# Norm factor moved behind the projections in a two-layer decode kernel

## Chip, cores, metric

The kernel runs on one core of a Trainium2 chip. The metric is device time in microseconds (us). Three runs of the kernel before spread over 0.3% (1176.41 to 1179.94 us), so a few us of 1177 need several runs. The sets of rounds ran on different chips, so compare kernels of different rounds by their ratios to the kernel before.

## The reference, cut to what matters

Two layers, each attention over a cache and then an mlp, for 8 rows of one token. Layernorm stands before every projection, twice in a row before the mlp's.

```python
def _layernorm(x, axis=-1, eps=1e-5):
    m = jnp.mean(x, axis=axis, keepdims=True)
    v = jnp.var(x, axis=axis, keepdims=True)
    return (x - m) / jnp.sqrt(v + eps)

def _A_ref(x, k_cache, v_cache, wq, wo):      # x [8,1,448], caches [8,8,4096,256] bf16
    q = (x @ wq) ...                          # 16 heads of 256
    p = softmax(einsum(q, k) / 16);  o = einsum(p, v)
    return o @ wo
def _B_ref(x, w1, w2, w3, w4):                # with one token the shifted branch adds zeros
    x1 = x + hs                               # hs = 0 here
    return x1 + _gelu(_layernorm(x1) @ w3) @ w4

x = x + _A_ref(_layernorm(x), ...);  x = x + _B_ref(_layernorm(x), ...)   # twice
```

## The kernel before

K and V come in chunks of 1 MB through a ring of five buffers (440 chunks in all). TensorE (PE) transposes K, VectorE (DVE) and ScalarE (ACT) copy the transposes out, PE makes scores and the product with V. Some K of a row stays on chip for the second layer, so that the two layers are interleaved: row b of layer 1 runs beside row b+1 of layer 0. The norm, queries and mlp of a row are generators ("jobs"). A piece of a job, up to its next `yield`, is put into the stream between pieces of attention. The traces show each engine's instructions in the order in which they are written (an example is the copy in the section "The copy to the upper partitions back on PE": it ran at 1167.25 us, with its input there since 1164.83).

The activations are 448 = 64 + 3 x 128 long. Only 64 partitions of the first chunk are used. Weights for that chunk are folded, half of their columns on partitions 0 to 63 and half on 64 to 127, so the second half of a projection needs the first chunk of activations on the upper partitions too. `lift` puts it there.

```python
def layernorm(lo, n, twice):            # n rows from lo
    ... squares, sums over chunks (2 DVE operations)
    op("pool", partition_all_reduce(sm[:, 1, 0:2*n], sm[:, 0, 0:2*n], P, add))
    yield; yield
    ... mean, variance, eps (5 DVE operations)
    yield
    ... (twice: 1), xc = x - mean (2)
    yield from rsqrt(2, 3, ...)         # 3 operations, then 3 Newton steps of 3
def lift(n):
    op("pe", matmul(mm[64:P, C_L:C_L+n], ident[0:64, 0:64], lnT[0:64, 0, 0:n]))
    op("dve", tensor_copy(lnT[64:P, KC, 0:n], mm[64:P, C_L:C_L+n]))
def mix(lo, n):                         # mlp; queries(lo, n) begins the same way
    yield from layernorm(lo, n, True)
    scaled(lnT, r_ln, 1, n)             # lnT = xc * factor, bf16
    scaled(t1, r_t1, 0, n); xres = x + t1
    for _ in range(WAIT): yield         # WAIT = 5
    for ts in (range(0, 2), range(2, 4), range(4, 7), ...):
        project(w3_cols, w3_r, C_H, ts, ts[0] >= NF // 2, n)
        if ts[0] == 0: lift(n)
        yield
    op("dve", tensor_copy(h_, mm[...])) # then gelu, w4, x = 0.5 * y + xres
```

There are 19 norms: 9 for queries (one for all eight rows at the start) and 10 for mlps. Near the end `outputs(0, 7)` and `mix(0, 7)` handle the second layer's rows 0 to 6 together, in the stream of row 7; `mix(7, 1)` runs last, with nothing beside it.

## Time and profile before

1177.4 us, median of 3 runs (1176.41 to 1179.94).

| stretch (us) | DMA GB/s | what limits it |
|---|---|---|
| 0 to 59 | 359, 391 | first loads and weights |
| 88 to 1000 | 415 | DMA (busy share 1.01) |
| 1110 to 1160 | 327 | ring buffers come free late (DMA's busy share 0.86) |
| after 1158.3 | about 0 | the last chunk has landed; a chain of small operations |

The profile page of the kernel before, the rows of 40 equal slices (tenths of busy time; granted PE clock in tenths; GB/s moved):

```profile
PE   2777898779877887778887887778887887878886
PEclk8979989999989999999989999999999999999987
DMA  9999999999999999999999999999999999999993
GB/s 359 391 415 419 419 396 417 418 420 412 417 416 420 411 418 410 420 420 404 420 404 420 415 412 416 420 409 412 419 417 420 416 405 417 412 420 414 407 335 133
```

No slice goes over 420 GB/s, and from 88 to 1000 us the mean busy share of the core's 16 DMA engines is 1.01, at 415 GB/s. The window view shows the same by stretch (stretch and length; then PE, weight loads, DVE, ACT and POOL busy us with instruction counts; granted clock, DMA share, GB/s):

```profile
88.00:1000.00 912.00, 741.12 (x15213) 645.35 (x15212) 387.50 (x1416) 252.66 (x726) 85.02 (x224) 0.96 1.01 415
1000.00:1110.00 110.00, 87.81 (x1913) 76.17 (x1911) 46.29 (x179) 29.25 (x87) 10.64 (x28) 0.98 1.01 416
1110.00:1160.00 50.00, 44.45 (x925) 37.47 (x921) 21.23 (x83) 12.17 (x35) 4.38 (x11) 0.90 0.86 327
```

The waits of the DMA's own queue (who waited for whom: us in total, times, longest):

```profile
SPq L123 <- PE tk L599: 451.4, 171, 5.3
SPq L123 <- PE pvb L697: 447.8, 235, 5.7
```

The queue waited about 900 us in all for PE to free a buffer. DMA therefore never runs further ahead than the ring's five buffers.

The tail, from the timeline of the kernel before (start us, duration us, engine, line, operation, output and inputs, shapes; in brackets the idle time before it and what ended it):

```profile
1162.67 0.41 POOL L343 PARTITION_ALL_REDUCE sm<-sm  x1 [4.56 <-DVE sm L339]
...
1166.58 0.16 DVE L330 SCALAR_TENSOR_TENSOR sm<-sm 128x2 f32<-128x2 f32 x1
1166.78 0.18 DVE L368 TENSOR_TENSOR lnT<-xc,sm 128x4 bf16<-128x4 f32 x1
...
1167.01 0.26 PE L409 MATMUL mm<-lnT,w_sb 128*128 128x24 bf16 x3 [5.03 <-DVE t L368]
...
1167.33 0.21 PE L396 MATMUL mm<-lnT,ident 64*64 64x1 bf16 x1
1167.58 0.17 DVE L399 CAST lnT<-mm 64x1 bf16<-64x1 f32 x1 [0.36 <-PE mm L396]
1167.80 0.26 PE L409 MATMUL mm<-lnT,w_sb 128*128 128x24 bf16 x3 [0.26 <-DVE lnT L399]
...
1169.30 0.18 DVE L493 COPY hb<-mm 128x14 f32<-128x14 f32 x1 [1.55 <-PE mm L409]
...
1173.78 0.38 DVE L775 COPY x_row<-tk 8x448 bf16<-8x448 bf16 x1 [0.72 <-PE tk L772]
```

Read it downward. After the POOL sum (ends 1163.08) VectorE works alone until 1166.96, then PE works, with a stop of 0.26 us for the lift's copy. The factor's chain on VectorE and the projection on PE do not overlap at all. From the end of the POOL sum to the end of the copy to `x_row` it is 11.07 us; I call this the tail interval below.

### The profile page before, as it was taken

Reading aid. Unit: us, or ns where it says so; the run is one execution under the profiler, and the core shown is the slowest. Engines: PE = TensorE matmul, PEld = TensorE weight load, DVE = VectorE, ACT = ScalarE, POOL = GpSimd, SP = SyncE. Lnnn points to the kernel's source line nnn. Section 1 sums busy time; section 2 is a strip of 40 time slices with the busy share of each in tenths; the row PEclk is TensorE's granted clock in tenths of the full one; section 3 lists DMA queues with packets and bytes.
Section 4 is the critical chain, followed back from the end, with each engine's and each line's share of the span. In section 5 each row is a group of like instructions: output and inputs, shape, how many; then the busy total and the mean of one; then the engine's idle time right before and its main releaser. Section 6 shows DMA issues by size and latency. Waiting matters only on the chain.

```text
span 1175.9 us, 42204 instructions
## 1 busy us (share of the span) xinstructions
PE 932.0 (79%) x19067; PEld 811.0 (69%) x19067; DVE 487.6 (41%) x1803; ACT 312.3 (27%) x891; POOL 105.4 (9%) x281
## 2 busy tenths in 40 slices
PE   2777898779877887778887887778887887878886
PEld 2666777668766776667776776667766776767675
DVE  2333543345333543345333543345333553345243
ACT  1223322222223222232222322223222222232121
POOL 0000001100100011000110001100110011000100
PEclk8979989999989999999989999999999999999987
DMA  9999999999999999999999999999999999999993
GB/s 359 391 415 419 419 396 417 418 420 412 417 416 420 411 418 410 420 420 404 420 404 420 415 412 416 420 409 412 419 417 420 416 405 417 412 420 414 407 335 133
DMA packets 70676, 474.66 MB, mean 404 GB/s; under 512 B 7248, under 2 KB 13280, under 8 KB 13792
## 3 DMA queue, kind: packets, MB, share of 16 engines
q1 hardware_dynamic: 70496, 471.97, 98.0%
q8 instruction: 149, 2.44, 0.8%
q14 instruction: 31, 0.25, 0.1%
HBM read 471.93 MB, written 0.01 MB: 401 GB/s over the span
## 4 chain that ended last, share of the span: by engine, by line
DMA 51%; PE 35%; DVE 8%; issue 4%; POOL 1%; ACT 0%; SPq 0%; POOLq 0%; ACTq 0%
DMA ring<-in_A_k_cache_dram 51%; PE tk L599 16%; PE ps L623 6%; PE pvb L697 5%; PE mm L449 3%; DVE ktr L606 2%; PE mm L409 2%; PE mm L513 1%; PE pvb L715 1%; DMA ring<-in_A_v_cache_dram 1%; DVE keep L606 1%; DVE oT L722 1%; DVE sm L347 1%; DVE os L718 0%; DVE sm L329 0%
## 5 line engine op out<-in xcount | busy, mean ns | idle before, releaser
L599 PE MATMUL tk<-ident,ring 128*128 128x128 f32 x2944 | 407.5, 291 | 134.0 <-DMA ring<-in_A_k_cache_dram 133.6
L599 PEld LDWEIGHTS tk<-ident,ring 128*128 128x128 f32 x2944 | 343.7, 149 | 177.5 <-DMA ring<-in_A_k_cache_dram 169.3
L606 DVE COPY ktr<-tk 128x512 f32<-128x512 f32 x224 | 153.8, 689 | 192.5 <-PE tk L599 192.4
L604 ACT COPY ktr<-tk 128x512 f32<-128x512 f32 x224 | 129.8, 586 | 323.1 <-PE tk L599 323.0
L697 PE MATMUL pvb<-ring,pT 128*2 128x256 bf16 x4096 | 160.5, 276 | 34.6 <-DMA ring<-in_A_v_cache_dram 22.7
L623 PE MATMUL ps<-qT,keep 128*128 128x48 bf16 x4608 | 159.9, 184 | 5.6 <-issue 4.6
L606 DVE COPY keep<-tk 128x512 f32<-128x512 f32 x144 | 99.5, 691 | 145.3 <-PE tk L599 144.6
L623 PEld LDWEIGHTS ps<-qT,keep 128*128 128x128 bf16 x4608 | 145.3, 97 | 17.6 <-issue 11.5
L604 ACT COPY keep<-tk 128x512 f32<-128x512 f32 x144 | 84.3, 586 | 251.7 <-PE tk L599 251.7
L679 ACT ACTIVATE pT<-ps,nb 128x32 bf16<-128x32 f32 x256 | 76.6, 299 | 268.9 <-DVE nb L675 221.7
L623 PE MATMUL ps<-qT,ktr 128*128 128x48 bf16 x3584 | 129.5, 184 | 17.8 <-DVE ktr L606 8.9
L623 PEld LDWEIGHTS ps<-qT,ktr 128*128 128x128 bf16 x3584 | 115.6, 97 | 29.0 <-DVE ktr L606 22.3
L673 POOL PARTITION_ALL_REDUCE gm<-pm x128 | 45.6, 356 | 796.8 <-DVE pm L670 796.8
L697 PEld LDWEIGHTS pvb<-ring,pT 128*2 128x2 bf16 x4096 | 75.8, 82 | 58.6 <-DMA ring<-in_A_v_cache_dram 27.2
L703 DVE COPY ob<-pvb 128x256 f32<-128x256 f32 x128 | 53.7, 420 | 46.2 <-PE pvb L697 45.6
L684 POOL PARTITION_ALL_REDUCE dn<-rs x128 | 51.2, 400 | 150.8 <-ACT pT L679 150.8
L449 PE MATMUL mm<-oT,wo_sb 128*128 128x24 bf16 (+1 forms) x1152 | 52.7, 187 | 9.5 <-DVE oT L722 4.7
L715 PE MATMUL pvb<-ident,ob 128*128 128x128 f32 x256 | 53.8, 293 | 7.8 <-DVE ob L703 7.5
L409 PE MATMUL mm<-lnT,wq_sb 128*128 128x24 bf16 x864 | 48.2, 184 | 12.9 <-DVE lnT L368 10.2
L670 DVE TENSOR_REDUCE pm<-ps 128x2 f32<-128x64 f32 x128 | 28.6, 224 | 69.1 <-PE ps L623 68.5
L449 PEld LDWEIGHTS mm<-oT,wo_sb 128*128 128x128 bf16 (+1 forms) x1152 | 42.3, 101 | 19.7 <-DVE oT L722 16.6
L409 PEld LDWEIGHTS mm<-lnT,wq_sb 128*128 128x128 bf16 x864 | 39.7, 98 | 22.3 <-DVE lnT L368 10.4
(70 smaller groups left out, 487.3 us busy)
## 6 DMA issues: line engine op xcount, KB each, us to landing
ring<-in_A_v_cache_dram SPq DMA_DIRECT2D x256, 1024.0 KB, 10.3
ring<-in_A_k_cache_dram SPq DMA_DIRECT2D x184, 1024.0 KB, 10.8
wo_sb<-in_A_wo_dram SPq DMA_DIRECT2D x1, 3584.0 KB, 25.6
wq_sb<-in_A_wq_dram SPq DMA_DIRECT2D x3, 1024.0 KB, 11.1
w_sb<-in_B_w_dram SPq DMA_DIRECT2D x1, 1568.0 KB, 20.1
w_sb<-in_B_w_dram SPq DMA_DIRECT2D x3, 448.0 KB, 12.7
wqf_sb<-in_A_wq_dram SPq DMA_DIRECT2D x2, 256.0 KB, 14.3
w3f_sb<-in_B_w_dram SPq DMA_DIRECT2D x2, 112.0 KB, 13.5
```

Source lines behind the costliest of these rows:

```text
L409: last = e.matmul(room(P, at + t * B, n), cols(kc, t), copies(rhs, n), start=(kc == 1), stop=(kc == 0), skip_group_check=True)
L449: last = e.matmul(room(w, C_P + c, 1), wo[:, t, row0(c):row0(c) + w], copies(oT[:, t // 2, t % 2, b:b + 1], 1), start=(t == 4 * h), stop=( ...
L599: last = e.transpose(bank[:, j * P:(j + 1) * P], src[:, 4 * (f % 4) + j, :].bitcast(f32), ident4[:, :])
L604: op("act", lambda e: e.copy(flat, bank[:, :]), reads=[r_bank], writes=[r_kt])
L606: op("dve", lambda e: e.tensor_copy(flat, bank[:, :]), reads=[r_bank], writes=[r_kt])
L623: last = e.matmul(pst[:, at:at + 2 * N_REP].rearrange("p (r j) -> p r j", j=2), kt(i, c), repeated(qT[:, b, c, 2 * h:2 * h + 2]), start=(c ...
L673: op("pool", lambda e: e.partition_all_reduce(gm[q][0][:, :], pm[q][0][:, :], P, ReduceOp.max), reads=[pm[q][1]], writes=[gm[q][1]])
L679: return e.activation(pT[q][0][:, :, :].rearrange("p i j -> p j i")[:, j, :], pst[:, C_S:C_S + 2 * NI].rearrange("p (i j) -> p j i", j=2)[ ...
L684: op("pool", lambda e: e.partition_all_reduce(dn[q][0][:, :], rs[q][0][:, :], P, ReduceOp.add), reads=[rs[q][1]], writes=[dn[q][1]])
L697: last = e.matmul(pvb[at:at + 2, 0:DH], pT[q][0][:, a * HALF + i, :], v[:, i, :], start=(a == 0 and i < 4), stop=(a == 1 and i >= HALF - 4 ...
L703: op("dve", lambda e: e.tensor_copy(ob[:, :], pvb[:, 0:DH]), reads=[r_pv], writes=[r_ob])
L715: last = e.transpose(pvb[:, DH + c * P:DH + (c + 1) * P], ob[:, c * P:(c + 1) * P], ident4[:, :])
```

## The change

The factor 1/sqrt(var + eps) is one number per row, so it can multiply the projection's result instead of its input. PE gets x less its mean as soon as the sum is there, and projects while VectorE computes the factor. The PE lift is replaced by two VectorE operations on 32 partitions each.

```diff
-WAIT = 5
+WAIT = 3
 def rsqrt(src, dst, n):
-    op("dve", tensor_single_scalar(hv, v, -0.5, mult))
     ...
-        op("dve", tensor_tensor(w, w, hv, mult))
+        op("dve", scalar_tensor_tensor(w, w, -0.5, v, mult, mult))
 def layernorm(lo, n, twice):
     ...
-    op("pool", partition_all_reduce(sm[:, 1, 0:2*n], sm[:, 0, 0:2*n], P, add))
+    op("pool", partition_all_reduce(sg[:, 0:2*n], sm[:, 0, 0:2*n], P, add))
     yield; yield
-    ... 5 operations; yield; (1); xc = x - mean (2)
+    centered(lnT, r_ln, lo, n)                       # lnT = x - sum/D, 2 operations
+    yield
+    ... 3 operations for variance and eps
+    for p in (0, 32):
+        op("dve", scalar_tensor_tensor(lnT[64+p:96+p, KC, 0:n], sg[p:p+32, 0:n], -1.0/D,
+                                       x_[p:p+32, 0, :], mult, add))
+    ... (twice: 2)
+    yield
     yield from rsqrt(2, 3, ...)
-def lift(n): ...
 # queries
-    qT = copy(mm)
+    qT = mm * factor
 # mix
-    h_ = copy(mm)
+    h_ = mm * factor
     ... gelu
+    centered(xc, ...); t1 = xc * factor; xres = x + t1     # was ahead of the projection
```

More of the change, by code (lines that the diff above doesn't have):

```diff
@@ L170, in decode_two_layers @@
     sm, r_sm = sb("sm", [P, 8, 2 * B], f32)
+    sg, r_sg = sb("sg", [P, 2 * B], f32)
     smi, r_smi = sb("smi", [P, 2 * B], i32)
@@ L196, in decode_two_layers @@
     C_Q = 160
-    C_L = 480
     C_P = 448
@@ L316, in rsqrt @@
     def rsqrt(src, dst, n):
-        v, y, w, hv = sm[:, src, 0:n], sm[:, dst, 0:n], sm[:, 7, 0:n], sm[:, 6, 0:n]
+        v, y, w = sm[:, src, 0:n], sm[:, dst, 0:n], sm[:, 7, 0:n]
         op("dve", lambda e: e.tensor_single_scalar(smi[:, 0:n], v.bitcast(i32), 1, ALU.arith_shift_right),
@@ L322, in rsqrt @@
            reads=[r_smi], writes=[r_smi])
-        op("dve", lambda e: e.tensor_single_scalar(hv, v, -0.5, ALU.mult), reads=[r_sm], writes=[r_sm])
         yield
@@ L328, in rsqrt @@
             op("dve", lambda e, a=a: e.tensor_tensor(w, a, a, ALU.mult), reads=[r_a], writes=[r_sm])
-            op("dve", lambda e: e.tensor_tensor(w, w, hv, ALU.mult), reads=[r_sm], writes=[r_sm])
+            op("dve", lambda e: e.scalar_tensor_tensor(w, w, -0.5, v, ALU.mult, ALU.mult), reads=[r_sm], writes=[r_sm])
             op("dve", lambda e, a=a: e.scalar_tensor_tensor(y, w, 1.5, a, ALU.add, ALU.mult),
@@ L342, in layernorm @@
            reads=[r_x], writes=[r_sm])
-        op("pool", lambda e: e.partition_all_reduce(sm[:, 1, 0:2 * n], sm[:, 0, 0:2 * n], P, ReduceOp.add),
-           reads=[r_sm], writes=[r_sm])
+        op("pool", lambda e: e.partition_all_reduce(sg[:, 0:2 * n], sm[:, 0, 0:2 * n], P, ReduceOp.add),
+           reads=[r_sm], writes=[r_sg])
         yield
         yield
-        one = lambda o, *a: op("dve", lambda e: e.tensor_single_scalar(o, *a), reads=[r_sm], writes=[r_sm])
-        one(sm[:, 1, 0:2 * n], sm[:, 1, 0:2 * n], 1.0 / D, ALU.mult)
@@ L349, in layernorm @@
-        op("dve", lambda e: e.scalar_tensor_tensor(s(2), s(1), -1.0, s(1), ALU.mult, ALU.mult),
-           reads=[r_sm], writes=[r_sm])
-        op("dve", lambda e: e.tensor_tensor(s(2), s(2), s(1, 1), ALU.add), reads=[r_sm], writes=[r_sm])
-        one(s(4), s(2), 0.0, ALU.max)
-        one(s(2), s(4), LN_EPS, ALU.add)
-        yield
+        centered(lnT, r_ln, lo, n)
+        yield
+        op("dve", lambda e: e.scalar_tensor_tensor(s(2), sg[:, 0:n], -1.0 / (D * D), sg[:, 0:n], ALU.mult, ALU.mult),
+           reads=[r_sg], writes=[r_sm])
@@ new lines, in layernorm @@
+        op("dve", lambda e: e.scalar_tensor_tensor(s(4), sg[:, n:2 * n], 1.0 / D, s(2), ALU.mult, ALU.add),
+           reads=[r_sg, r_sm], writes=[r_sm])
+        op("dve", lambda e: e.tensor_scalar(s(2), s(4), 0.0, LN_EPS, ALU.max, ALU.add), reads=[r_sm], writes=[r_sm])
+        for p in (0, 32):
+            op("dve", lambda e, p=p: e.scalar_tensor_tensor(
+                lnT[64 + p:96 + p, KC, 0:n], sg[p:p + 32, 0:n], -1.0 / D, x_[p:p + 32, 0, :], ALU.mult, ALU.add),
+               reads=[r_x, r_sg], writes=[r_lift])
@@ L355, in layernorm, with centered @@
         if twice:
+            op("dve", lambda e: e.tensor_single_scalar(s(4), s(4), 0.0, ALU.max), reads=[r_sm], writes=[r_sm])
             op("dve", lambda e: e.scalar_tensor_tensor(s(2, 1), s(2), LN_EPS, s(4), ALU.mult, ALU.add),
                reads=[r_sm], writes=[r_sm])
+        yield
+        yield from rsqrt(2, 3, 2 * n if twice else n)
+    def centered(dst, r_dst, lo, n):
         for hi, c0, c1 in ((P, 1, 4), (64, 0, 1)):
-            op("dve", lambda e, hi=hi, c0=c0, c1=c1: e.tensor_tensor(
-                xc[0:hi, c0:c1, 0:n], x_[0:hi, c0:c1, :],
-                s(1)[0:hi].unsqueeze(1).to_broadcast([hi, c1 - c0, n]), ALU.subtract),
-               reads=[r_x, r_sm], writes=[r_xc])
@@ L365, in layernorm @@
-        yield from rsqrt(2, 3, 2 * n if twice else n)
-    def scaled(dst, r_dst, a, n):
-        op("dve", lambda e: e.tensor_tensor(dst[:, 0:KC, 0:n], xc[:, :, 0:n],
-                                            bc(sm[:, 3, a * n:(a + 1) * n], n), ALU.mult),
-           reads=[r_xc, r_sm], writes=[r_dst])
+            op("dve", lambda e, hi=hi, c0=c0, c1=c1: e.scalar_tensor_tensor(
+                dst[0:hi, c0:c1, 0:n], sg[0:hi, 0:n].unsqueeze(1).to_broadcast([hi, c1 - c0, n]), -1.0 / D,
+                xT[0:hi, c0:c1, lo:lo + n], ALU.mult, ALU.add),
+               reads=[r_x, r_sg], writes=[r_dst])
@@ L392, in w3_cols @@
         return w3f[:, t % (NF // 2) * P:(t % (NF // 2) + 1) * P]
-    def lift(n):
-        op("pe", lambda e: e.matmul(mm[64:P, C_L:C_L + n], ident[0:64, 0:64], lnT[0:64, 0, 0:n],
-                                    start=True, stop=True, skip_group_check=True),
-           reads=[r_ident, r_ln], writes=[r_mm])
-        op("dve", lambda e: e.tensor_copy(lnT[64:P, KC, 0:n], mm[64:P, C_L:C_L + n]),
-           reads=[r_mm], writes=[r_lift])
     def project(cols, r_w, at, ts, upper, n):
@@ L416, in queries @@
         yield from layernorm(lo, n, False)
-        scaled(lnT, r_ln, 0, n)
         for _ in range(WAIT):
@@ L422, in queries @@
                 project(wq_cols, wq_r, C_Q, range(t, t + 2), t >= 16, n)
-                if t == 0:
-                    lift(n)
                 yield
@@ L427, in queries @@
                 continue
-            op("dve", lambda e, h=h: e.tensor_copy(
+            op("dve", lambda e, h=h: e.tensor_tensor(
                 qT[:, lo, :, 2 * h:2 * h + 2],
-                mm[:, C_Q + 4 * h * B:C_Q + 4 * (h + 1) * B].rearrange("p (a c n) -> p n c a", n=B, c=2)[:, 0, :, :]),
-               reads=[r_mm], writes=[r_q[lo][h]])
+                mm[:, C_Q + 4 * h * B:C_Q + 4 * (h + 1) * B].rearrange("p (a c n) -> p n c a", n=B, c=2)[:, 0, :, :],
+                sm[:, 3, 0:1].unsqueeze(2).to_broadcast([P, 2, 2]), ALU.mult),
+               reads=[r_mm, r_sm], writes=[r_q[lo][h]])
             ready[lo] = h + 1
@@ L436, in queries @@
             if n > 1:
-                op("dve", lambda e, c=c: e.tensor_copy(
+                op("dve", lambda e, c=c: e.tensor_tensor(
                     qT[:, lo:lo + n, c, :],
-                    mm[:, C_Q:C_Q + 32 * B].rearrange("p (a c n) -> p n c a", n=B, c=2)[:, 0:n, c, :]),
-                   reads=[r_mm], writes=[r for b in range(lo, lo + n) for r in r_q[b]])
+                    mm[:, C_Q:C_Q + 32 * B].rearrange("p (a c n) -> p n c a", n=B, c=2)[:, 0:n, c, :],
+                    sm[:, 3, 0:n].unsqueeze(2).to_broadcast([P, n, HQ]), ALU.mult),
+                   reads=[r_mm, r_sm], writes=[r for b in range(lo, lo + n) for r in r_q[b]])
     def output(b, h):
@@ L479, in mix @@
         yield from layernorm(lo, n, True)
-        scaled(lnT, r_ln, 1, n)
-        scaled(t1, r_t1, 0, n)
-        op("dve", lambda e: e.tensor_tensor(xres[:, :, 0:n], x_, t1[:, :, 0:n], ALU.add),
-           reads=[r_x, r_t1], writes=[r_xres])
         for _ in range(WAIT):
@@ L488, in mix @@
             project(w3_cols, w3_r, C_H, ts, ts[0] >= NF // 2, n)
-            if ts[0] == 0:
-                lift(n)
             yield
         h_, w_ = hb[:, :, 0:n], hw[:, :, 0:n]
-        op("dve", lambda e: e.tensor_copy(
-            h_, mm[:, C_H:C_H + NF * B].rearrange("p (t n) -> p t n", n=B)[:, :, 0:n]),
-           reads=[r_mm], writes=[r_hb])
+        op("dve", lambda e: e.tensor_tensor(
+            h_, mm[:, C_H:C_H + NF * B].rearrange("p (t n) -> p t n", n=B)[:, :, 0:n],
+            sm[:, 3, n:2 * n].unsqueeze(1).to_broadcast([P, NF, n]), ALU.mult),
+           reads=[r_mm, r_sm], writes=[r_hb])
         op("dve", lambda e: e.scalar_tensor_tensor(w_, h_, GELU_C, h_, ALU.mult, ALU.mult),
@@ L506, in mix @@
         yield
+        centered(xc, r_xc, lo, n)
+        op("dve", lambda e: e.tensor_tensor(t1[:, :, 0:n], xc[:, :, 0:n], bc(sm[:, 3, 0:n], n), ALU.mult),
+           reads=[r_xc, r_sm], writes=[r_t1])
+        op("dve", lambda e: e.tensor_tensor(xres[:, :, 0:n], x_, t1[:, :, 0:n], ALU.add),
+           reads=[r_x, r_t1], writes=[r_xres])
         yield
```

## The prediction

> **What bounds the kernel now.** Input. The page shows 474.66 MB moved at a mean of 404 GB/s and the DMA row at 9 in all slices but the last; between 88 and 1000 us the window view gives 415 GB/s. [...] no 29 us slice of the trace goes over 420. The DMA queue's own waits agree: about 900 us for PE to free ring buffers. Three stretches are different: the start (359 and 391 GB/s), 1110 to 1158 us (331 to 393 GB/s, buffers freed late by PE), and the tail after the last chunk has landed (1158.3 us).
>
> **What the change does.** In each of 17 norms (8 queries, 9 mlps) it takes the factor 1/sqrt(var) out of the way of the projection: x less mean goes to lnT right after the POOL sum, PE projects while VectorE does the Newton steps, and the factor is applied where PSUM is copied out anyway. Two 32-partition VectorE operations replace the PE lift (a 0.2 us matmul, and VectorE's wait for it: 11.8 us over 13 waits). The count of VectorE operations hardly changes (about 26 per mlp); each costs 0.16 us busy, and 0.197 us from start to start when it needs the one before. Each job has one step less.
>
> **What of it is critical, by the timeline.**
> - Tail. The last mlp runs alone. Before: POOL ends 1163.08, lnT 1166.78, first projection 1167.01, lift stall until 1167.80, hb copied at 1169.30. After: centred by about 1163.5, PE projects (about 2 us at half clock) until about 1165.8, hidden behind VectorE; 18 dependent operations at 0.197 us with a few overlaps put the factor at about 1166.7, so hb is at 1166.7. Saves about 2.6 us. The residual's four operations hide behind the 2.2 us of w4 matmuls.
> - Start. The POOL sum still comes at 21.2. Queries before: 26.4 to 31.25. After: PE from 22.0, factor at about 26.1, scores at about 27 rather than 31.3. But the DMA queue is full until wo has landed (42.3 us), and PE waits for K again at 46 us. Gain: 0 to 0.5 us.
> - Middle, 15 norms: DMA stays at 418 GB/s but for dips of about 1 us at each batch change. About 1 us either way.
> - 1110 to 1158 us: some 7 us of DMA time are lost to late buffers, partly in a 2 us PE stall behind 11 norm operations (1128 to 1130). After, two neighbouring steps have 9 of them. Gain 0 to 1.5, loss possible.
>
> Sum: 2.6 + 0.2 + 0.6 = 3.4 us.
>
> **Predicted: 1174.0 us, 1170.8 to 1176.8 eight times in ten; faster by over 2% 0.01, within 2% 0.98, slower by over 2% 0.01.**
>
> **What would show it.** From the end of the last POOL sum to the end of x_row's copy 8.5 us, not 11.1; first score matmul at about 27 us and still a wait for K near 46 us; DMA rate between 88 and 1000 us unchanged at 415; no lift matmul; last chunk landing within 1.5 us of 1158.3.
>
> **What would make it wrong.** The last mlps shift so that the ring is refilled later or earlier in the final 50 us (several us either way); the 32-partition operations across partitions cost much more than 0.2 us; the step in which seven norm operations run in one piece stalls PE and the ring; the start does carry over to the DMA (up to 4 us).

Read from the trace: the half clock is the granted clock of 0.50 from 1162 to 1169.3 us; for the full queue speaks a DMA share of 1.01 to 1.09 in every 4 us from 20 to 44 us; the dips of about 1 us are an estimate from the slices (404 rather than 418 GB/s over 29.4 us are 1.0 us); so are the 7 us of lost DMA time, from the share of 0.86 over the 50 us from 1110 us.

## The result, and the profile after

1174.95 us, median of 4 runs (1171.94 to 1175.57), against 1177.49 us (1176.41 to 1179.94, 4 runs). The ratio is 0.997 with a 95% interval of 0.9947 to 0.9994. A second set of rounds (below) gave 1174.49 us and a ratio of 0.9966 (0.9949 to 0.9982). The output is correct.

The page of the changed kernel, the same rows:

```profile
PEclk8879999999999998899989998999988999999978
DMA  9999999999999999999999999999999999999984
GB/s 353 389 415 420 419 404 414 420 419 419 398 421 419 415 418 411 410 420 420 411 415 411 419 415 414 417 416 402 420 414 420 417 414 405 419 420 415 408 325 176
```

And its windows:

```profile
88.00:1000.00 912.00, 745.88 (x15224) 651.05 (x15223) 386.85 (x1398) 253.67 (x727) 85.10 (x224) 0.96 1.01 415
1000.00:1110.00 110.00, 86.39 (x1898) 75.19 (x1895) 45.53 (x175) 28.51 (x86) 10.64 (x28) 0.98 1.01 418
1110.00:1160.00 50.00, 44.32 (x918) 38.28 (x917) 21.14 (x83) 12.18 (x35) 4.37 (x11) 0.86 0.87 329
```

Until 1160 us nothing moved that these views show: 415 GB/s again in the long stretch, 329 rather than 327 in the last one. The tail did move. The timeline of the changed kernel:

```profile
1162.80 0.41 POOL L342 PARTITION_ALL_REDUCE sg<-sm  x1 [4.49 <-DVE sm L338]
1163.24 0.36 DVE L370 SCALAR_TENSOR_TENSOR lnT<-sg,xx 128x3 bf16<-128x3 f32 x2 [0.54 <-POOL sg L342]
...
1163.66 0.26 PE L404 MATMUL mm<-lnT,w_sb 128*128 128x24 bf16 x3 [1.56 <-DVE lnT L370]
...
1164.07 0.34 DVE L356 SCALAR_TENSOR_TENSOR lnT<-sg,xx 32x1 bf16<-32x1 f32 x2
...
1165.21 0.18 PE L404 MATMUL mm<-lnT,w3f_sb 128*128 128x24 bf16 x1
...
1166.79 0.16 DVE L329 SCALAR_TENSOR_TENSOR sm<-sm 128x2 f32<-128x2 f32 x1
1167.06 0.18 DVE L480 TENSOR_TENSOR hb<-mm,sm 128x14 f32<-128x14 f32 x1
...
1171.55 0.38 DVE L769 COPY x_row<-tk 8x448 bf16<-8x448 bf16 x1 [0.72 <-PE tk L766]
```

PE starts 0.45 us after the sum's end and is through at 1165.4, long before the factor (1166.95). `hb` follows the factor at once. The factor itself comes no sooner, 3.74 us after the sum's end against 3.66 before: what is gained is overlap. The tail interval is 8.72 us, 2.35 less than before. The copies across partitions take 0.34 us for two. The move to other partitions cost nothing that this trace shows: 154 ns mean for a one-row copy (32x1, 34 of them) against 155 ns for the operation on 64x1 that stays on its partitions.

To see where the rest of the time stands, I read from the trace when each of the 440 ring chunks had landed (the last of its 16 completions). Time before, and what is to be added for the changed kernel and for three runs of the next section:

```
chunk   before    changed   ten ops,  ten ops,  two Newton
           us               one step  spread    steps
    7     44.7      +0.5      +0.6      +0.6      +0.4
   40    137.3      +0.6      +1.3      +0.7      +0.7
   60    188.8      +0.2      +8.4      +4.2      +0.4
  200    544.8      +0.5     +13.8      +7.2       0.0
  320    850.0      +0.7     +24.7     +13.5      +1.0
  400   1053.3      +0.4     +28.9     +17.0      +0.8
  423   1111.9      +0.4     +29.5     +17.4      +0.8
  431   1133.1      +2.3     +31.6     +21.8      +1.7
  439   1158.3      +0.3     +31.7     +19.9      +3.0
```

For the changed kernel every chunk lands within 3 us of the kernel before, nearly all within 1 us, and the last one 0.3 us later. At the start the first 64 score matmuls began at 27.90 us rather than 31.31 (in spite of a POOL sum that came 0.85 us later in this run). The kernel before, then the changed one:

```profile
31.31 2.90 PE L623 MATMUL ps<-qT,keep 128*128 128x48 bf16 x64 [0.71 <-DVE qT L437]
```

```profile
27.90 2.74 PE L617 MATMUL ps<-qT,keep 128*128 128x48 bf16 x64 [1.38 <-DVE qT L430]
```

Chunk 7, the first one issued after them, was issued 2.6 us earlier (33.60 rather than 36.20 us) but landed no earlier (45.2 and 44.7 us). These 3.4 us do not reach the loads. I read this as a DMA queue that was still full: the DMA share was 0.99 to 1.09 in every 4 us from 20 to 44 us of the changed kernel, and that issue took 4.31 us rather than 1.15.

### The profile page after: what moved, and what is told of

Read it like the earlier page. It is cut to its first block, busy times and chain, and to the rows that moved or that the text cites. A ratio compares the mean times of both kernels' runs of the same rounds, so it can differ in the third digit from the quotient of the medians.

```text
span 1173.6 us, 42148 instructions
## 1 busy us (share of the span) xinstructions
PE 937.8 (80%) x19048; PEld 819.3 (70%) x19048; DVE 486.0 (41%) x1776; ACT 312.3 (27%) x891; POOL 105.5 (9%) x281
## 4 chain that ended last, share of the span: by engine, by line
DMA 50%; PE 36%; DVE 8%; issue 4%; ACT 1%; POOL 1%; SPq 0%; POOLq 0%; DVEq 0%; ACTq 0%
DMA ring<-in_A_k_cache_dram 48%; PE tk L593 17%; PE ps L617 7%; PE pvb L691 5%; PE mm L443 3%; DVE ktr L600 2%; DMA ring<-in_A_v_cache_dram 2%; PE mm L404 2%; PE mm L507 1%; PE pvb L709 1%; DVE oT L716 1%; DVE os L712 1%; ACT ktr L598 0%; POOL gm L667 0%; DVE keep L600 0%
## 5 line engine op out<-in xcount | busy, mean ns | idle before, releaser
L593 PE MATMUL tk<-ident,ring 128*128 128x128 f32 x2944 | 418.8, 296 | 133.3 <-DMA ring<-in_A_k_cache_dram 133.2
L593 PEld LDWEIGHTS tk<-ident,ring 128*128 128x128 f32 x2944 | 352.5, 151 | 178.9 <-DMA ring<-in_A_k_cache_dram 170.0
```

What stands on the lines that cost most here:

```text
L593: last = e.transpose(bank[:, j * P:(j + 1) * P], src[:, 4 * (f % 4) + j, :].bitcast(f32), ident4[:, :])
```

## Experiments

My theory A was: only the tail pays, because the rest goes at the DMA's rate. Rival B: the earlier norms pay, with fewer stalls of PE and the ring. One correction to my own expectations first: they say "16 norms but the last" (and one says "all 17"); there are 18, and 19 in all.

### One half each

Both forms of the norm in one file, with a switch by norm. In the traces VectorE, ScalarE, GpSimd and PE run the same operations in the same order as the kernel before (t1) or the changed one (t2) up to the last norm.

```diff
+def is_new(kind, last): return last          # t1: new form in the very last mlp alone
+def is_new(kind, last): return not last      # t2: old form in the very last mlp alone
```

> The kernel before, with the new form of the norm in the very last mlp alone. Theory A (the gain lies in the tail after the last landing, because the rest runs at the DMA's rate): 2.4 us under the kernel before, ratio about 0.998; from the end of the last POOL sum to the end of the copy to x_row 8.7 us rather than 11.1; the last chunk lands within 1 us of the kernel before. Rival B (the gain comes from the 16 earlier norms: fewer stalls of PE and of the ring): less than 0.5 us under the kernel before in the part before the last landing plus 2.4 us is not B; B expects the same time as before, with a tail gain given back.

> The changed kernel, with the old form of the norm in the very last mlp alone. Theory A: within 0.7 us of the kernel before (ratio 0.9994 to 1.0006), tail interval 11.1 us as before, last chunk landing as before to 1 us. Rival B: about 2.5 us under the kernel before, with the last chunk landing that much earlier.

Measured: t1 1176.05 us (ratio 0.9982, 0.9963 to 1.0), tail interval 8.74 us. t2 1176.09 us (0.9984, 0.9966 to 1.0003), tail interval 11.08 us. The kernel before had 1178.37 us in these rounds. The tail does what A says in both. The times don't decide about the rest. t2 should have been within 0.7 us of the kernel before by A; it was 1.9 us under it, with an interval of about 2 us either way. Its last chunk landed 0.7 us earlier than in the kernel before; t1's landed 2.5 us later, and some of its earlier chunks up to 3.5 us later, though up to the last norm t1 and the kernel before are the same program. So single landings say nothing below some 3.5 us, and the small entries of the table above are neither gain nor loss.

### Ten more operations, in the last norm or in all others

```diff
         yield
+        if last:                              # t4; "if not last" in t3
+            for _ in range(10):
+                op("dve", tensor_single_scalar(s(4), s(4), 1.0, mult))    # each needs the one before
         yield from rsqrt(2, 3, ...)
```

> The changed kernel with ten more dependent small VectorE operations in the last norm alone. Theory A: all 2.0 us (ten times 0.197 us) show in the time: tail interval 10.7 us, time 0.4 us under the kernel before. Rival B: no rise over the changed kernel of more than 0.5 us.

> The changed kernel with ten more dependent small VectorE operations (about 2.0 us) in each of the 16 norms but the last, the first queries included: 32 us of VectorE chain added. Theory A: at most 1 us over the changed kernel, so still 1.5 to 2.5 us under the kernel before. Rival B: over the changed kernel by 4 us or more, so over the kernel before.

Measured: t4 1177.62 us (ratio 0.9996, 0.9977 to 1.0015), tail interval 10.60 us; the 1.9 us that were added to the tail are all there. t3 was 1203.58 us (ratio 1.021, 1.0183 to 1.0238). That is 29 us over the changed kernel (by the medians; 28 by the ratios), 1.6 us for each norm. Theory A, as I had put it ("at most 1 us"), fell here. The trace of t3 at the first change of rows. First VectorE's timeline, then PE's:

```profile
157.71 1.83 DVE L367 TENSOR_SCALAR sm<-sm 128x1 f32<-128x1 f32 x10
...
159.83 0.68 DVE L603 COPY ktr<-tk 128x512 f32<-128x512 f32 x1
```

```profile
157.78 0.44 PE L712 MATMUL pvb<-ident,ob 128*128 128x128 f32 x2
160.57 0.57 PE L620 MATMUL ps<-qT,ktr 128*128 128x48 bf16 x16 [2.36 <-DVE ktr L603]
162.96 0.83 PE L446 MATMUL mm<-oT,wo_sb 128*64 128x24 bf16 x16 [1.82 <-DVE oT L719]
```

And the windows of t3 there:

```profile
155.00:160.00 5.00, 3.16 (x42) 2.40 (x42) 3.64 (x24) 1.72 (x6) 1.05 (x3) 1.00 1.02 416
160.00:165.00 5.00, 2.62 (x64) 2.15 (x64) 2.79 (x14) 0.00 (x0) 0.00 (x0) 0.78 0.97 406
165.00:170.00 5.00, 5.00 (x62) 4.50 (x55) 1.45 (x3) 0.97 (x2) 0.00 (x0) 0.54 0.68 226
```

The eviction of a transpose (VectorE's copy of it out of PSUM) stands behind the ten operations on VectorE. PE waits 2.36 us for it, then 1.82 us for the next result. The changed kernel at the same change of rows:

```profile
155.44 0.57 PE L617 MATMUL ps<-qT,ktr 128*128 128x48 bf16 x16 [0.42 <-DVE sm L327]
157.83 0.72 PE L443 MATMUL mm<-oT,wo_sb 128*64 128x24 bf16 x16 [1.81 <-DVE oT L716]
```

So the second wait was there already, and the first is the new one. Over this stretch VectorE's copies fall behind those of the changed kernel in two steps, one at each norm's ten operations: from 0.7 us (at 129 us) to 3.2 (at 150), and to 6.2 (at 170).

After the two waits PE's granted clock falls to 0.54, and although PE is busy all of the 5 us from 165, the ring is refilled at 226 GB/s. In the tail of the kernel before, where PE waited 5.03 us, it was 0.50; what makes it fall was not tested. But the low clock is not peculiar to t3. The kernel before has it at the same change of rows (0.58, with a refill at 362 GB/s), and its chunk 60 landed 0.2 us earlier than the changed kernel's:

```profile
160.00:165.00 5.00, 5.00 (x67) 4.71 (x60) 1.59 (x4) 1.17 (x2) 0.00 (x0) 0.58 0.96 362
```

So the low clock alone is not the cause; what it adds to the two delays was not separated. The landings above show the result: no delay to speak of by 137 us, 8.4 us by 189 us, and more at the later changes of rows.

### The same ten operations, spread

Was it the unbroken 2 us, or the sum? Two of the ten operations in each of five steps:

```diff
+    def more():                               # two small dependent operations
+        for _ in range(2):
+            op("dve", tensor_single_scalar(sm[:, 5, 0:1], sm[:, 5, 0:1], 1.0, mult))
# called after centered(), after the integer part of rsqrt and after each Newton step, not in the last norm;
# a memset of sm at the start is left out here
```

> The changed kernel with the same ten extra small VectorE operations per norm (all but the last), but two in each of five steps of the norm instead of ten in one step. Theory Block (what cost 27 us in the run with ten in one piece is a VectorE that is deaf for 2 us, so that PE stalls behind an eviction): at most 10 us over the changed kernel. Theory Total (VectorE work near a batch change costs time one for one, wherever it stands): 20 us or more over it.

The changed kernel was run unedited in the same rounds:

> The changed kernel, unedited, as the reference point for this chip and these rounds: about 3 us under the kernel before (ratio 0.997 to 0.998), tail interval 8.7 us.

Measured: u1 1174.49 us (ratio 0.9966, 0.9949 to 0.9982), tail 8.71 us. u2 1194.78 us (ratio 1.0142, 1.0123 to 1.0162), 20.3 us over u1, 1.1 us for each norm. Most of the cost stays when the work is spread, so the sum of VectorE work near a change of rows counts more than its lumps: Block does not fit, and Total fits its bound, just above 20 us, though not "one for one", which would be 36. The lump adds some 8 us (the intervals of t3's and u2's ratios do not overlap). Why just 1.1 of 2.0 us per norm come through I have not taken apart. A lower granted clock is not needed for it: in the profiled executions it is 0.940 over u2 and 0.936 over u1, and u2's last chunk is 20 us later all the same. Over all runs u2's mean is the lower one, 0.933 against 0.943, so a share of the clock stays open.

### Three operations fewer

If adding costs that much, does taking away pay?

```diff
-        for i in range(3):        # Newton steps
+        for i in range(2):
```

> The changed kernel with two Newton steps rather than three in every norm (three VectorE operations, 0.6 us, out of all 17). Theory Ceiling (before the last landing nothing can be gained, since the DMA already runs at its rate but for about 1 us per batch): 0.6 us from the tail (tail interval 8.1 us) and at most 1.5 us more. Theory Slope (the middle's norms cost in proportion both ways, as the ten extra operations cost 1.7 us per norm for 2 us of work): 0.5 us per norm, about 8 us under the changed kernel. The result stays correct either way.

Measured: 1177.13 us (ratio 0.9995, 0.998 to 1.001), correct, 2.6 us over u1. The tail interval fell to 8.13 us as forecast, but the last chunk landed at 1161.32. The landings (last column above) are those of the changed kernel up to 1112 us and slip in the last 45 us. The single landing could be chance, but not the time: the six runs of u3 (1176.26 to 1178.83) and the six of u1 (1170.82 to 1175.11) do not overlap. One Newton step also held one `yield`, so all that follows in a job had moved by a step. The next run takes out the operations and keeps the step:

```diff
-        for i in range(3):
+        for i in range(2):
             ...
             yield
+        yield
```

> As the run with two Newton steps, but the scheduling step that went with the third is kept, so every later piece of a norm's job stands where it stands in the changed kernel. If that run lost its gain because its jobs moved by a step in the last 45 us (its chunks landed within 0.3 us of the changed kernel's up to 1112 us and 2.7 us late at the end), the last chunk now lands within 1 us of the changed kernel's and the time is 0.6 us under it (the tail, 8.1 us). If fewer VectorE operations themselves did harm, it is again about 2.6 us over it.

Measured: 1173.45 us (ratio 0.9962, 0.9949 to 0.9974), last chunk at 1158.31 us, tail 8.13 us. Its ratio's interval lies below u3's. So the 3 us were lost by the dropped step and not by the missing operations; that it is the place of the last pieces is what u3's landings suggest. And both runs show that 0.6 us less VectorE work in every norm brings no chunk in earlier (within about 1 us of the changed kernel's up to 1112 us, where Slope forecast some 8): the middle has a ceiling above and a slope below.

### The copy to the upper partitions back on PE

```diff
-        for p in (0, 32): op("dve", scalar_tensor_tensor(lnT[64+p:96+p, KC, 0:n], ...))
+    # lift(n) as before, after the first projection step
```

> The changed kernel with the copy of the first chunk back on PE (matmul with the identity, then one VectorE cast), nothing else undone. If the copy by VectorE carries none of the gain (theory: the gain is the factor taken off the chain), time and tail (8.7 us, at most 0.3 us more) are those of the changed kernel to 1 us. If it does, 1 us or more over it, and the tail 0.5 us longer.

Measured: 1176.49 us (ratio 0.9989, 0.9976 to 1.0002), tail interval 10.00 us, 1.28 over the changed kernel's. The theory that the copy carries none of the gain was wrong for the tail; the times (ratio 0.997 for the changed kernel in other rounds) overlap and do not decide. The timeline of this run:

```profile
1164.62 0.21 PE L396 MATMUL mm<-lnT,ident 64*64 64x1 bf16 x1
...
1167.08 0.16 DVE L330 SCALAR_TENSOR_TENSOR sm<-sm 128x2 f32<-128x2 f32 x1
1167.25 0.17 DVE L399 CAST lnT<-mm 64x1 bf16<-64x1 f32 x1
1167.47 0.26 PE L409 MATMUL mm<-lnT,w_sb 128*128 128x24 bf16 x3 [2.65 <-DVE lnT L399]
```

The lift matmul is done at 1164.8, but its VectorE half is written after the Newton steps, so it runs after them (at 1167.25, with its input there since 1164.83), and PE stands still for 2.65 us. The factor out of PE's way gains 1.07 us of the tail without the copy on VectorE; the copy, written ahead of the Newton steps, brings the other 1.28 of the 2.35. It is the place that counts here: a PE lift whose VectorE half is also written ahead of the Newton steps was not run and could do as well.

### The waiting steps

```diff
-WAIT = 3
+WAIT = 5
```

> The changed kernel with five waiting steps rather than three. The middle and the tail stay the same (chunks within 1 us up to 1112 us, tail 8.7 us); only the place of the last mlps' pieces in the final stream moves by two steps, so that the last chunk may land up to 3 us earlier or later: within 3 us of the changed kernel, direction not known.

Measured: 1175.08 us (ratio 0.9981, 0.9968 to 0.9995), tail 8.72 us (so the waiting steps play no part in the tail's gain), middle unchanged. The profiled execution had its last chunk at 1155.12 us, 3 us early, but from there to the end of the last POOL sum it took 5.9 us rather than 4.6 in the changed kernel, and the times don't show a gain; against the changed kernel (0.9966) the intervals overlap. Inconclusive, within about 3 us.

### One mlp at the end

The last 50 us before 1160 run at 327 to 329 GB/s. PE and VectorE do an mlp of seven rows there. The last mlp could take all eight:

```diff
         elif b == B - 2:
-            jobs.extend([outputs(0, B - 1), mix(0, B - 1)])
+            jobs.append(outputs(0, B - 1))
         elif b == B - 1:
-            jobs.append(mix(B - 1, 1))
+            jobs.append(mix(0, B))
```

> The changed kernel, but the mlp of the second layer's rows 0 to 6 no longer runs during the last stream; all eight rows go through one mlp at the end. From 1110 to 1150 us PE loses 112 matmuls (about 4.5 us) and VectorE some 26 operations; the tail's VectorE operations are wider (tail interval 9.3 to 9.5 us rather than 8.7). If the slow DMA between 1110 and 1150 us comes from that mlp, the last chunk lands 2 to 5 us earlier and the time falls 1.5 to 4 us under the changed kernel; if it comes from the attention's own chain there, the landing is the same and the time rises by 0.7 us.

The 4.5 us are an estimate: in the tail of the kernel before, at a granted clock of 0.50, the projection of the last mlp kept PE busy for 1.99 us and its 56 matmuls with w4 for 2.16 us.

Measured: 1172.20 us (range 1171.91 to 1173.81; ratio 0.9954, 0.994 to 0.9968). The window view of this run, over the same stretches as above and then within the last one:

```profile
1110.00:1160.00 50.00, 42.85 (x841) 36.58 (x840) 17.50 (x58) 11.76 (x34) 3.77 (x10) 0.87 0.85 336
```

```profile
1110.00:1130.00 20.00, 18.35 (x413) 16.17 (x416) 5.75 (x21) 3.74 (x12) 1.51 (x4) 0.83 0.90 343
1130.00:1150.00 20.00, 17.38 (x310) 15.24 (x299) 8.09 (x22) 6.09 (x16) 1.51 (x4) 0.91 1.00 409
1150.00:1160.00 10.00, 7.12 (x132) 5.18 (x130) 3.66 (x15) 1.93 (x6) 0.75 (x2) 0.86 0.43 178
```

For comparison, the changed kernel:

```profile
1130.00:1150.00 20.00, 18.42 (x382) 16.43 (x383) 10.20 (x40) 5.47 (x16) 1.33 (x4) 0.91 0.95 344
```

With the mlp gone from there, DMA is back at 409 GB/s from 1130 to 1150 us (344 in the changed kernel, 350 in u1 of the same rounds). But that is not the mlp alone: with the mlp in place w4 had this:

```profile
1130.00:1150.00 20.00, 18.40 (x398) 16.19 (x394) 12.06 (x49) 6.18 (x17) 1.54 (x4) 1.00 0.97 384
```

Over the whole 50 us u4 and u1 both moved 336 GB/s. The last chunk landed at 1156.52 us, 1.7 us before u1's, which is within the scatter of landings, and the wider operations cost the tail 0.63 us (9.35). Both together, with two Newton steps and the step kept:

> The kernel with one mlp for all eight rows at the end, with two Newton steps and the scheduling step kept. Tail interval 8.75 us rather than 9.35, last chunk landing as in the kernel with the merged mlp to 1 us (about 1156.5): 1171.6 us, the fastest so far, ratio to the kernel before about 0.995.

Measured: 1172.48 us (ratio 0.9956, 0.9944 to 0.9969), last chunk 1154.79 us, tail 8.71 us. The 0.6 us of the tail are in the profile, but the time is no lower than with three Newton steps. The first merged kernel has a median 2.3 us under the changed one's of the same rounds, but a mean only 1.4 us under it (the ranges overlap), and the second had no such neighbour in its rounds; the intervals of the ratios overlap with the changed kernel's. So a gain of the merged mlp over the changed kernel is not shown. Against the kernel before, both gain some 5 us clear of noise.

## Why the prediction was right, and where it was not

- **The time.** 1174.0 us forecast, 1174.95 and 1174.49 measured, both in the range. Forecast gain 3.4 us; the ratios give 3.5 and 4.0 us (0.7 to 6.2 and 2.1 to 6.0 by their intervals). The range was 6 us wide and would have held any gain from 0.7 to 6.7 us, so the time alone proves little; the tail intervals carry the account.
- **Tail: right.** 2.6 us forecast, 2.35 measured (11.07 to 8.72). `hb` started 3.85 us after the end of the sum, where 3.6 was counted. Shown by t1, t2 and t4 as well: the tail interval goes with the form of the last norm, and added operations come through whole.
- **Start: right.** Scores began at 27.90 us, forecast about 27; the chunks landed no earlier.
- **Middle and last 50 us: right in that little came, and not resolved in size.** 0.8 us was forecast ahead of the last norm, 0.2 of it at the start. Four comparisons, each with about 2 us of uncertainty, give what the changed program gains ahead of its last norm: time gained over the kernel before, less the tail's part. They are 1.2 (first rounds), 1.6 (u1), 1.9 (t2) and 0.0 us (t4), mean 1.2; t2 and t4 share their runs of the kernel before. This is in line with the forecast, but not clear of zero, and which place it would come from is open.
- **Counts: wrong.** I wrote 17 norms, 8 and 9; there are 19, 9 and 10 (the forms for 7 and 8 rows had been left out). It did not matter to the sum.
- **A step that was thin:** "DMA stays at 418 GB/s but for dips of about 1 us at each batch change ... about 1 us either way". I take it that this holds for this change only because it leaves the count of VectorE operations near a change of rows as it was. The runs show that this place gained nothing when 0.6 us was taken out of every norm, but lost 1.1 to 1.6 us for each 2 us added. I had taken a stretch with a saturated DMA (share 1.01, 415 GB/s) to have slack; it has almost none.
- **The lift** was costed as a stall of about 0.5 us. Within the new order it is worth 1.28 us of the tail.

## What to carry to other kernels

A per-row factor that only scales a matmul's result belongs behind the matmul, but here it paid only where nothing else covers the chain: 2.35 us in the last 10 us of a run that has DMA at 415 GB/s through most of it, and 1.2 us, not clear of zero, elsewhere. All that PE waits for must then also be written ahead of the factor's chain on an engine whose trace shows the written order, as VectorE's does: half of the tail's gain (1.28 of 2.35 us) hung on the place of one small copy. And a saturated DMA doesn't prove slack elsewhere: test it by adding work (2 us per norm cost 1.1 to 1.6 here), since taking work away may show nothing (0.6 us less per norm brought no chunk in earlier).

## Measured here besides

- Small VectorE operations: the float operations of the norms, of one or two elements, took 146 to 161 ns in the changed kernel, in their means by kind and shape (the reduction of eight elements to two: 168 ns). From start to start of small operations that need each other it was 0.195 us in the Newton steps of the last norm (eight steps from 1165.23 to 1166.79).
- Waits of PE and its granted clock: in t3 two waits of 2.36 and 1.82 us, with 0.57 us of work between them, the second up to 162.96 us, came before a clock of 0.54 (165 to 170 us). In the changed kernel waits of 0.42 and 1.81 us, the second up to 157.83 us, came before 3.3 us at 0.50 (from 159.2 us).
- The ring: with five 1 MB buffers and DMA at 415 GB/s, 2 us of VectorE work more for each of 18 norms cost 20 to 29 us.
